# Seven products of halves in place of eight for the up projections of the second expert network

## The chip, the core and the metric

One core of a Trainium2 chip runs the whole program. The metric is device time in microseconds (us) from the first to the last instruction of one execution, with what lies around it. The engines are TensorE (PE; its weight loads are listed apart as PEld), VectorE (DVE), ScalarE (ACT), GpSimd (POOL) and SyncE (SP), which issues the DMAs.

## What is computed

Attention with a bucket mask on 2 batches of 768 tokens, then a first network, then a second one with 4 experts. Only the second network is computed in another way; `x` is the output of the first, 1536 tokens by 512.

```
h = x @ w_in ; x = (h - tanh(h)) @ w_out          # first network, d_ff = 2048
out = zeros(1536, 512)                            # second network, E = 4, F = 1024
for e in range(4):
    h = maximum(x @ w1[e], 0.0)                   # up projection, 512 -> 1024
    out += p[:, e:e+1] * (h @ w2[e])              # down projection, 1024 -> 512
```

## The kernel before

**Products in three passes.** Each 32-bit operand of the two networks is split into a high part (rounded to fp32r) and a low part (the rest), as a tile of two planes. One product of a 128x128 block with 512 columns is three matmuls: high by high, high by low, low by high. Each matmul has a weight load of its own in the PE queue.

**First network and attention: a list scheduler.** All steps up to the end of the first network are entered with `add` in a `Plan`: for each step a priority, the engines that may run it with a cost, what it reads and writes, and the buffers ("slots") that it holds. `Plan.order` then plays the steps against these costs and so fixes the order in which each engine's queue is written. At run time the engines follow these queues in order and wait on semaphores.

**Second network: written out in order.** After the planned part a plain loop follows, over experts `e`, chunks `c` of 512 tokens and blocks `fb` of 128 hidden units (4 x 3 x 8 = 96 rounds). A round has 12 matmuls for the up projection into a PSUM bank `ph` (L268 in `up_steps`: 4 blocks of the contraction by 3 passes), ACT's Relu (L959) and DVE's low part (L960) of the hidden values `hb`, and 12 matmuls for the down projection into four PSUM banks `acc` (L936). The weight blocks are split anew in every round: ACT makes the high part (L918), POOL the low part (L919). The banks `acc` sum over the 8 blocks of an expert, so DVE adds to the output only once per expert and chunk (L974, L978: 4 x 3 x 4 = 48 instructions). The output leaves by one DMA for each 128 tokens (L983). Between first and second network, ACT and DVE split the sums of the first network into high and low parts of `x` (L273, L276).

Of the kernel before, what the change touches and what calls it, by code (L numbers as in the profile page):

```python
# [16 lines left out]
P = 128  # L17
# [8 lines left out]
E = 4  # L26
# [14 lines left out]
NG = 4  # L41
NTH = 9
FILL = 8
# [169 lines left out]
def attn_moe_kernel(ctx: ExitStack, tc: tile.TileContext, qk, v, proj, ident, wa, wb, dp, out):  # L213
# [7 lines left out]
    fpa = pool("fpa", NF1)  # L221
    rwp = pool("rwp", 2)
    wps = [pool("wp0", 2)]
    hp = pool("hp", NG)
    tp2 = pool("tp2", NTH)
    apa = pool("apa", KB4)
# [15 lines left out]
    def f_tile(p):  # L242
        return p.tile([P, CH], F32, tag="f", name="f")

    def raw_tile(p):
        return p.tile([P, CH, 2], U32, tag="raw", name="raw")
# [39 lines left out]
    def banks(n, name, shape=(P, CH)):  # L286
        return tiles(n, list(shape), F32, name, pp)

    gs_ = [pair(hp, "g") for i in range(NG)]
# [19 lines left out]
        f=[f_tile(fpa) for i in range(NF1)],  # L309
        fo=[],  # L310
        raw=[raw_tile(rwp) for i in range(2)],
# [3 lines left out]
        xp=[pair(apa, "a") for kb in range(KB4)],  # L315

        g=gs_[0 : NG // 2],
        th=[tp2.tile([P, CH], F32, tag="th", name="th") for i in range(NTH)]
        + [t[:, j, :].bitcast(F32) for t in gs_[NG // 2 :] for j in range(2)],

# [4 lines left out]
        acc=[],  # L325
    )
# [400 lines left out]

    def make_xT(c, kb, p):

        pt, t = ("up", "pt", c, kb), ("xp", 1, c, kb)  # L730
# [6 lines left out]
        add(p, {TE: (0.43, turn)}, x + [("id32",)], [pt], [t])  # L737
        split(p + 0.1, lambda: pl[t], lambda: pl[pt], [pt], ("xT", c, kb), [t], psum=True)

    def network_up(c, fb, p, cut):  # L740
# [5 lines left out]
        def step(m):  # L746
            if not m:
                steps.update(enumerate(up_steps(pl[ph], pl[w], [pl["xp", 1, c, kb] for kb in range(KB4)])))
            steps[m]()

        for m in range(3 * KB4):
            add(p, {TE: (0.227, lambda m=m: step(m))},
                ks + [(("xT", c, kb), i) for kb in range(KB4) for i in ("hi", "lo")], [ph],
                [w] + [("xp", 1, c, kb) for kb in range(KB4)])
# [3 lines left out]
    def network_down(c, fb, p, cut):  # L758
# [4 lines left out]
        for db in range(4):  # L763
            add(p, {TE: (0.68, lambda db=db: down(
                pl["acc", c, db], pl[v_], pl[g], db, fb == 0, fb == NF1 - 1
            ))}, ks + gs, [("acc", c, db)], [v_, g])

# [45 lines left out]
    for i in range(SHORT):  # L813
        k = ("po", "fill", i)
        add(2e5 + i, {TE: (0.11, lambda k=k: nc.tensor.matmul(pl[k][:, 0:256], warm[:, 0:P], warm[:, 0:256], start=True, stop=True))}, (), (), [k])

# [13 lines left out]
    for c in range(NC):  # L830
# [4 lines left out]
        for db in range(4):  # L835
            split(down_at(c, NF1) - 8, lambda c=c, db=db: pl["xp", 2, c, db], lambda c=c, db=db: pl["acc", c, db],
                  [("acc", c, db)], ("x2", c, db), [("xp", 2, c, db)], psum=True)
            pl.users["xp", 2, c, db] += 1
    dps = cp.tile([P, NT // P, E], F32, name="dps")
    dsum = cp.tile([P, NT // P, 1], F32, name="dsum")  # L840
    pw = cp.tile([P, NT // P, E], F32, name="pw")
    k = [("pw",)]
    dma(330, lambda: dps, lambda: dp.rearrange("(t p) e -> p t e", p=P), w=k, lat=0.67, after=exps[-1:])
    for f in (
        lambda: nc.vector.tensor_reduce(out=dsum, in_=dps, axis=AX.X, op=ALU.add),
        lambda: nc.vector.tensor_scalar(out=dsum, in0=dsum, scalar1=1e-9, scalar2=None, op0=ALU.add),
        lambda: nc.vector.reciprocal(out=dsum, in_=dsum),
        lambda: nc.vector.tensor_tensor(out=pw, in0=dps, in1=dsum.to_broadcast([P, NT // P, E]), op=ALU.mult),
    ):
        add(331, {VE: (0.12, f)}, k, k)  # L850
    apb, fpb = [], []


# [27 lines left out]


    new = {"fo": [Slot() for i in range(NF1)], "xp": [Slot() for i in range(2 * KB4)], "raw": [Slot() for i in range(NRQ)], "wd": [Slot() for i in range(2)]}

    def switch():
        actx.close()
        wps.append(pool("wp1", 2, reuse_waits="tile"))
        rwq = pool("rwq", NRQ, reuse_waits="tile")
        apb.append(pool("apb", 2 * KB4, reuse_waits="tile"))
        fpb.append(pool("fpb", NF1, reuse_waits="tile"))  # L890
# [146 lines left out]
```

## Time and profile before

| what | value |
|---|---|
| median of 3 runs | 1003.62 us (1000.98 to 1003.82) |
| the profiled execution | 1003.25 us, of which the span of its trace is 1001.5 us |
| PE busy over the span | 986.8 us (99%), 6326 matmuls |
| PEld / DVE / ACT / POOL busy | 787.1 / 460.6 / 468.8 / 501.4 us |
| second network, 475.10 to 997.60 us of the span | 522.50 us, 2304 matmuls |

Matmuls overlap: the time of one in the table of groups is from its issue to its modelled end, so a stretch is priced by its length over the number of its matmuls and not by the mean of one. DVE and ACT rows overlap too, by some 0.08 to 0.12 us, when they stand back to back.

### The profile page before, as it was taken

To read this page: it belongs to the slowest core of one execution; us is meant where nothing else is said; L and a number is where in the kernel's file an instruction comes from. 1 tells how busy PE (TensorE), PEld (TensorE's weight loads), DVE (VectorE), ACT (ScalarE), POOL (GpSimd) and SP (SyncE) were. 2 spreads that over 40 slices of the span, in tenths; PEclk is the share of its full clock that TensorE was granted. 3 is DMA by queue.
4 is the path that set the end of the run, shared out by engine and by line. 5 is a ranking of instruction groups with operands and counts; after the bars stand their busy time and mean duration, and the time that the engine had idled before them with its cause. 6 is when DMAs were issued, how large, how long until landed. Compare 5 with 4: busy or idle time off the path is not lost.

```text
span 1001.5 us, 16255 instructions
## 1 busy us (share of the span) xinstructions
PE 986.8 (99%) x6326; PEld 787.1 (79%) x6326; DVE 460.6 (46%) x807; ACT 468.8 (47%) x941; POOL 501.4 (50%) x385
## 2 busy tenths in 40 slices
PE   8999999999999999999999999999999999999998
PEld 4766766677888888888888888888888888888886
DVE  8998998998987544444121212122121211212122
ACT  7898979887544433433333333333333333333331
POOL 3675757863654133356445444454444544444442
PEclk9999999999999999999999999999999999999999
DMA  6422243223330011123000220001300000001011
GB/s 198 128 86 81 80 145 99 78 73 114 117 116 22 22 41 44 54 84 94 1 1 1 74 85 11 1 0 53 95 21 1 1 1 1 0 1 43 1 43 42
DMA packets 32114, 53.85 MB, mean 54 GB/s; under 512 B 6150, under 2 KB 11174, under 8 KB 32038
## 3 DMA queue, kind: packets, MB, share of 16 engines
q1 hardware_dynamic: 32038, 52.83, 17.2%
q8 instruction: 49, 0.80, 0.4%
q14 instruction: 27, 0.22, 0.1%
HBM read 43.18 MB, written 3.15 MB: 46 GB/s over the span
## 4 chain that ended last, share of the span: by engine, by line
PE 89%; DVE 4%; ACT 2%; DMA 2%; issue 1%; POOL 1%; SPq 1%; POOLq 0%; DVEq 0%; ACTq 0%
PE ph L268 26%; PE acc L936 26%; PE st L255 7%; PE sf L255 7%; PE sf L268 6%; PE po L268 4%; PE st L268 2%; PE st L599 2%; PE st L604 2%; PE sf L515 2%; DVE mx L521 2%; PE po L652 1%; PE po L651 1%; PE po L653 1%; PE sf L484 1%
## 5 line engine op out<-in xcount | busy, mean ns | idle before, releaser
L919 POOL TENSOR_TENSOR w<-f,w 128x512 fp32r<-128x512 f32 x192 | 247.5, 1289 | 280.4 <-ACT w L918 280.4
L268 PE MATMUL ph<-a,w 128*128 128x512 f32 x1152 | 276.6, 389 | 0.1
L936 PE MATMUL acc<-w,hb 128*128 128x512 f32 x1152 | 276.5, 389 | 0.0
L960 DVE SCALAR_TENSOR_TENSOR hb<-ph,hb 128x512 fp32r<-128x512 f32 x96 | 66.4, 692 | 421.8 <-ACT hb L959 421.8
L268 PEld LDWEIGHTS ph<-a,w 128*128 128x128 f32 x1152 | 216.1, 188 | 45.4 <-PE st L255 0.5
L936 PEld LDWEIGHTS acc<-w,hb 128*128 128x128 f32 x1152 | 216.2, 188 | 44.9
L918 ACT ACTIVATE w<-f 128x512 fp32r<-128x512 f32 x192 | 120.5, 628 | 161.0 <-PE acc L936 108.6
L959 ACT ACTIVATE hb<-ph 128x512 fp32r<-128x512 f32 x96 | 57.4, 598 | 194.6 <-PE ph L268 194.6
L276 POOL TENSOR_TENSOR w<-f,w 128x512 fp32r<-128x512 f32 x57 | 88.4, 1551 | 114.0 <-ACT w L273 109.3
L276 POOL TENSOR_TENSOR ph<-p,ph 128x768 f16<-128x768 f32 x56 | 95.3, 1716 | 46.0 <-ACT ph L610 32.0
L521 DVE TENSOR_REDUCE mx<-sf 128x1 f32<-128x384 f32 x192 | 98.6, 549 | 9.2 <-PE sf L515 8.4
L273 ACT ACTIVATE w<-f 128x512 fp32r<-128x512 f32 x90 | 56.8, 632 | 79.7 <-PE st L255 71.4
L610 ACT ACTIVATE ph<-st 128x384 f16<-128x384 f32 x192 | 92.4, 504 | 3.1 <-PE st L604 2.8
L268 PE MATMUL sf<-a,w 128*128 128x512 f32 x288 | 77.6, 408 | 0.0
L610 ACT ACTIVATE p<-st 128x384 f32<-128x384 f32 x144 | 72.0, 500 | 5.3 <-PE st L604 4.8
L255 PE MATMUL sf<-g,w 128*128 128x512 f32 x288 | 73.8, 390 | 0.1
L255 PE MATMUL st<-g,w 128*128 128x512 f32 x288 | 73.1, 389 | 0.0
L711 POOL TENSOR_TENSOR f<-f,raw 128x512 uint32<-128x512 uint32 x32 | 48.1, 1505 | 38.0 <-DVE f L708 29.9
L599 PE MATMUL st<-qk 97*128 97x384 f16 x192 | 62.9, 327 | 2.5 <-DMA qk<-mt 1.8
L255 PEld LDWEIGHTS sf<-g,w 128*128 128x128 f32 x288 | 53.9, 188 | 11.6 <-DVE w L276 0.5
L255 PEld LDWEIGHTS st<-g,w 128*128 128x128 f32 x288 | 54.1, 188 | 11.3
L604 PE MATMUL st<-qk 128*128 128x384 f16 x192 | 62.7, 326 | 0.0
(121 smaller groups left out, 1208.0 us busy)
## 6 DMA issues: line engine op xcount, KB each, us to landing
raw<-wa SPq DMA_DIRECT2D x64, 256.0 KB
f<-wb SPq DMA_DIRECT2D x64, 256.0 KB
r<-qk SPq DMA_DIRECT2D x15, 384.0 KB
qk<-qk SPq DMA_DIRECT2D x60, 96.0 KB
vr<-v SPq DMA_DIRECT2D x8, 384.0 KB
out<-oacc SPq DMA_DIRECT2D x12, 256.0 KB
qk<-bt SPq DMA_DIRECT2D x56, 9.0 KB
r<-qk SPq DMA_DIRECT2D x2, 192.0 KB
```

Of the source, the lines that this page charges most:

```text
L255: nc.tensor.matmul(acc, a, g[:, i, :], start=(first and n == 0), stop=(last and n == 2))
L268: nc.tensor.matmul(ph, a, xt[kb][:, i, :], start=(m == 0), stop=(m == n - 1))
L276: return lambda: eng.tensor_tensor(out=dst(), in0=a(), in1=b(), op=ALU.subtract)
L521: nc.vector.tensor_reduce(out=pl["mx", h][:, qt, j : j + 1], in_=pl[ps][:, 0:384], axis=AX.X, op=ALU.max)
L599: nc.tensor.matmul(ps[j][:, 0:384], t[0:97, KB, kt * P : kt * P + P], t[0:97, QA, j * 384 : j * 384 + 384], start=True, stop=False,)
L604: nc.tensor.matmul(ps[j][:, 0:384], t[:, KC, kt * P : kt * P + P], t[:, QC, j * 384 : j * 384 + 384], start=False, stop=True,)
L610: nc.scalar.activation(o.rearrange("p (a b) -> p a b", a=2)[:, js[0]], pl[st][:, 0:384], AF.Exp, scale=1.0 / (8.0 * SC * SC),)
L918: nc.scalar.activation(w[:, 0], f, AF.Copy)
L919: nc.gpsimd.tensor_tensor(out=w[:, 1], in0=f, in1=w[:, 0].bitcast(F32), op=ALU.subtract)
L936: nc.tensor.matmul(acc[tt], a, w[:, i, :], start=(first and n == 0), stop=(last and n == 2))
L959: nc.scalar.activation(hb[:, 0, :], ph, AF.Relu)
L960: nc.vector.scalar_tensor_tensor(out=hb[:, 1, :], in0=ph, scalar=0.0, in1=hb[:, 0, :].bitcast(F32), op0=ALU.max, op1=ALU.subtract)
```

## The change

The 1024 hidden units of an expert are taken in pairs of blocks (16 pairs `u` over the experts), the contraction in two halves of 256, and the tokens of a batch `b` in two halves of `HN` = 384. The up projection of one pair and one batch is then a 2x2 by 2x2 block product. It is computed with seven block products in place of eight (the form of Strassen's algorithm with shared sums): four sums of weight halves (`stationary`), four sums of token halves (`moving`), seven products of 6 matmuls with 384 columns each (`product`), and seven additions on DVE (`plus`) that put the four hidden blocks together. These additions read a product's PSUM bank and one of three SBUF tiles `rs`. The hidden blocks are split as before (`hidden`). The down projection has the same matmuls, but its bank `dn` sums over the two blocks of a pair alone, so DVE adds to the output after every pair: 16 x 2 x 6 = 192 instructions. The steps of the second network are entered in the same `Plan` as the rest; its buffers lie where those of attention and the first network lay (`gives_later` and `hand` pass them on). The output of the first network is now copied to SBUF by ACT before it is summed and split.

```diff
+    def moving(b, p):
...
+        def cut_(o, src, i, j, r, use, p):
...
+            sums[b].append(add(p, {AC: (0.05 + n * 0.92e-3, act_copy(hi, src))}, r, [(k, "hi")], [bo[o], *use]))
+            sums[b].append(both(
+                p + 0.1, sub(nc.vector, lo, src, h32), sub(nc.gpsimd, lo, src, h32), n, [*r, (k, "hi")], [(k, "lo")], [bo[o], *use]
+            ))
...
+        for n, halves, x, y, o in ((0, (1, 0), (0, 0), (0, 1), 3), (1, (1,), (1, 0), 0, 4), (2, (0,), (1, 0), 1, 6), (3, (1, 1), (1, 0), (0, 1), 5)):
...
+    def stationary(u, p):
...
+        for n, (op, x, y, r) in enumerate((
+            (ALU.add, a21, a22, [w[1]]), (ALU.subtract, s_(0), a11, [("s", u, 0), w[0]]),
+            (ALU.subtract, a11, a21, w), (ALU.subtract, a12, s_(1), [("s", u, 1), w[0]]),
+        )):
...
+    def step2(u, b, p, q):
...
+        def product(pm, a, o):
+            def f():
+                n = 0
+                for k in range(2):
+                    hi, lo = (pl[ao][:, a, i, k * P : k * P + P] for i in range(2))
+                    for x, i in ((hi, 0), (hi, 1), (lo, 0)):
+                        nc.tensor.matmul(bank(o), x, pl["bo%d" % b, o][:, k, i, :], start=(n == 0), stop=(n == 5))
+                        n += 1
...
+        def plus(pm, o, n, to=None):
+
+            dst = (lambda: bank(o)) if to is None else (lambda: pl[rs[to]])
+            add(p + pm, {VE: (0.465, lambda: nc.vector.tensor_tensor(out=dst(), in0=bank(o), in1=pl[rs[n]], op=ALU.add))},
+                [ch[o], rs[n]], [ch[o] if to is None else rs[to]])
...
+        product(0, 0, 0)
+        add(p + 0.5, {AC: (0.37, act_copy(lambda: pl[rs[0]], lambda: bank(0)))}, [ch[0]], [rs[0]])
+        product(1, 1, 1)
+        plus(1.5, 1, 0)
+        hidden(1.6, 1, 0, 0)
+        product(2, 4, 4)
+        plus(2.5, 4, 0, 0)
+        product(4, 5, 5)
+        plus(4.5, 5, 0, 1)
+        product(6, 3, 3)
+        plus(6.5, 3, 0, 0)
+        plus(6.6, 3, 1)
+        hidden(6.7, 3, 1, 1)
+        product(8, 2, 6)
+        plus(8.5, 6, 1)
+        hidden(8.6, 6, 1, 0)
+        product(10, 6, 2)
+        plus(10.5, 2, 0)
+        hidden(10.6, 2, 0, 1)
+        for t in range(2 * HN // P):
...
+                f = lambda dn=dn, o=o, sc=sc: nc.vector.scalar_tensor_tensor(
+                    out=o(), in0=pl[dn], scalar=sc, in1=o(), op0=ALU.mult, op1=ALU.add
+                )
...
+            add(down_at(c, NF1) - 8, {AC: (0.48, lambda c=c, db=db: nc.scalar.activation(
+                xs[c][:, db, :], pl["acc", c, db], AF.Copy
+            ))}, [("acc", c, db)], [("x2", c, db)], after=turns[c] + (sums[0] if c == 2 else []))
...
+    gives_later("rs", 2, lambda: [part(hp2_t, 2 * CH + HN * i, HN) for i in range(2)], net)
...
+    for n in range(2):
+        hand("wu", n, "w2", False, ups2)
+    for n in range(4):
+        hand("up", n, "ch", False, ups2)
+        hand("acc", n, "ch" if n < 2 else "dn", False, net)
...
-    for e in range(E):
-        for c in range(NC):
-            for fb in range(NF2):
...
-                ph = up(split_w(we2[fb, 0], 0), x2[c])
```

In the rows below, line numbers of the kernel before are those of the profile; in the rows of the change L919 is a matmul of `product`, L974 a matmul of the down projection, L930 is `plus`, L940 the low part in `hidden`, L984 the addition to the output, L294 a subtraction (a low part or a sum of halves). The tiles `ab`, `xa`, `fb`, `rq`, `rw` hold the split token halves, `fa` the split weight sums, `tp` and `hp` the split hidden blocks, `hp_87` and `fb_4470` are `rs`, `xs` holds `x`, its sums and later the output. PSUM banks keep the names of attention (`sf`, `st`, `po`).

Where the last down projection of the first network (L255) ends, PE's queue had the first rounds of the second network:

```order
L255 MATMUL st_167<-g,w 128x512 x3
L255 MATMUL st_168<-g,w 128x512 x3
L268 MATMUL ph<-a,w 128x512 x24
L936 MATMUL acc_6028<-w,hb 128x512 x3
L936 MATMUL acc_6029<-w,hb 128x512 x3
```

Now seven products stand there between the last down projection of the first network (L273 in the change's numbering, same banks) and the first of the second; four products of batch 0 have moved ahead of it, in among the first network's last 11 blocks:

```order
L273 MATMUL st_145<-hp,w 128x512 x3
L273 MATMUL st_146<-hp,w 128x512 x3
L919 MATMUL sf_149<-rq,fa 128x384 x6
L919 MATMUL sf_148<-ab,fa 128x384 x6
L919 MATMUL po_151<-rw,fa 128x384 x6
L919 MATMUL po_150<-xa,fa 128x384 x6
L919 MATMUL st_144<-xa,fa 128x384 x6
L919 MATMUL po_150<-fb,fa 128x384 x6
L919 MATMUL sf_147<-fb,fa 128x384 x6
L974 MATMUL st_145<-w,tp 128x512 x6
```

The rounds with their up projection first are gone from here; the first down projection of the second network comes after seven products in place of 24 matmuls.

At the same place DVE's queue had the four low parts of the last chunk of `x` and went on with one instruction a round:

```order
L276 TENSOR_TENSOR a<-sf_171,a 128x512
L276 TENSOR_TENSOR a<-sf_170,a 128x512
L276 TENSOR_TENSOR a<-st_167,a 128x512
L276 TENSOR_TENSOR a<-st_168,a 128x512
L960 SCALAR_TENSOR_TENSOR hb<-ph,hb 128x512 x9
```

Now 22 instructions stand between the first sum of token halves and the last low part of batch 0's hidden blocks. The first nine are two sums of 512 and 256 elements, a sum of 768, three low parts of 768 (all for batch 1), a `plus` of batch 0, the low part of a weight block (512) and another sum of 768; these are the next twelve:

```order
L940 SCALAR_TENSOR_TENSOR tp<-po_150,tp 128x384
L294 TENSOR_TENSOR fb<-xs_99,fb 128x2x384
L930 TENSOR_TENSOR hp_87<-st_144,hp_87 128x384
L294 TENSOR_TENSOR w<-hp_87,w 128x512
L930 TENSOR_TENSOR fb_4470<-sf_147,hp_87 128x384
L294 TENSOR_TENSOR fb<-xs_99,fb 128x2x384
L930 TENSOR_TENSOR hp_87<-sf_149,hp_87 128x384
L930 TENSOR_TENSOR sf_148<-sf_148,fb_4470 128x384
L930 TENSOR_TENSOR sf_149<-sf_149,fb_4470 128x384
L930 TENSOR_TENSOR po_151<-po_151,hp_87 128x384
L940 SCALAR_TENSOR_TENSOR tp<-sf_148,tp 128x384
L940 SCALAR_TENSOR_TENSOR tp<-sf_149,tp 128x384
```

The additions of batch 0 have come in among the splits for batch 1; the low part in the last of these rows is one that the first down projection of the second network reads.

In the middle of the second network, where PE's queue repeated 12 matmuls L268 and 12 matmuls L936, one step (one pair, one batch) begins so; the down projections are those of the step before:

```order
L919 MATMUL sf_149<-ab,fa 128x384 x6
L919 MATMUL st_144<-ab,fa 128x384 x6
L919 MATMUL po_151<-ab,fa 128x384 x6
L974 MATMUL st_145<-w,tp 128x512 x3
L974 MATMUL st_145<-w,hp 128x512 x3
L919 MATMUL po_150<-ab,fa 128x384 x6
L974 MATMUL st_146<-w,tp 128x512 x3
L974 MATMUL st_146<-w,hp 128x512 x3
L919 MATMUL sf_147<-rq,fa 128x384 x6
```

It goes on in turn with down projections three and four and the last two products, and ends with down projections five and six side by side. The two banks of the down projection, `st_145` and `st_146`, alternate; products use the other six banks.

## Rows read from the trace of the kernel before

**Rows 1.** The page: span, busy time of PE, and the span in 40 slices.

```profile
span 1001.5 us, 16255 instructions
...
PE   8999999999999999999999999999999999999998
...
PEclk9999999999999999999999999999999999999999
```

**Rows 2.** Busy time by stretch: us, then each engine's busy us, PE clock, DMA.

```profile
475.10:997.60 522.50, 522.48 (x2304) 432.34 (x2304) 98.61 (x145) 166.66 (x286) 243.59 (x189) 1.00 0.07 21
```

**Rows 3.** Groups by line and shape: count | busy us, mean ns | idle before.

```profile
L268 PE MATMUL ph<-a,w 128*128 128x512 f32 x1152 | 276.6, 389 | 0.1
L936 PE MATMUL acc<-w,hb 128*128 128x512 f32 x1152 | 276.5, 389 | 0.0
L268 PEld LDWEIGHTS ph<-a,w 128*128 128x128 f32 x1152 | 216.1, 188 | 45.4 <-PE st L255 0.5
```

**Rows 4.** Timeline of PE, f16 matmuls alone: start us, us from first start to last end.

```profile
182.24 0.33 PE L599 MATMUL st<-qk 97*128 97x384 f16 x1
182.41 0.33 PE L604 MATMUL st<-qk 128*128 128x384 f16 x1
```

**Rows 5.** Timeline of PE, a 384-column matmul followed by 32-bit weights (two places).

```profile
182.57 0.33 PE L515 MATMUL sf<-qk 96*128 96x384 f16 x1
182.60 0.76 PE L268 MATMUL sf<-a,w 128*128 128x512 f32 x2
183.19 0.34 PE L515 MATMUL sf<-qk 96*128 96x384 f16 x1
...
156.09 0.34 PE L515 MATMUL sf<-qk 96*128 96x384 f16 x1
156.13 1.00 PE L268 MATMUL sf<-a,w 128*128 128x512 f32 x3
156.97 0.34 PE L599 MATMUL st<-qk 97*128 97x384 f16 x1
```

**Rows 6.** Timeline of the weight loads: 32-bit ones that follow each other closely.

```profile
182.57 0.36 PEld L268 LDWEIGHTS sf<-a,w 128*128 128x128 f32 x2
...
250.04 0.47 PEld L734 LDWEIGHTS st<-id,xs 128*128 128x128 f32 x4
```

**Rows 7.** Timeline of DVE: back-to-back rows of 384 and of 512 elements.

```profile
101.54 1.94 DVE L521 TENSOR_REDUCE mx<-sf 128x1 f32<-128x384 f32 x4
...
995.60 2.79 DVE L978 SCALAR_TENSOR_TENSOR oacc<-acc,pw,oacc 128x512 f32<-128x512 f32 x4 [2.08 <-PE acc L936]
```

**Rows 8.** Groups of DVE, ACT and POOL whose shapes are near those of the change.

```profile
L626 DVE TENSOR_TENSOR ph<-st,ph 128x384 f16<-128x384 f32 x48 | 24.5, 548 | 0.6 <-ACT st L623 0.4
L276 DVE TENSOR_TENSOR ph<-p,ph 128x768 f16<-128x768 f32 x16 | 16.5, 1035 | 2.3 <-ACT ph L610 2.3
L276 DVE TENSOR_TENSOR g<-th,g 128x512 fp32r<-128x512 f32 x36 | 26.2, 727 | 1.3 <-ACT g L273 0.5
L276 DVE TENSOR_TENSOR w<-f,w 128x512 fp32r<-128x512 f32 x39 | 31.9, 819 | 4.2 <-ACT w L273 2.2 <-POOL f L711 1.2 <-DVE w L719 0.5
L623 ACT ACTIVATE st<-st 128x384 f32<-128x384 f32 x48 | 21.9, 499 | 0.0
L919 POOL TENSOR_TENSOR w<-f,w 128x512 fp32r<-128x512 f32 x192 | 247.5, 1289 | 280.4 <-ACT w L918 280.4
L276 POOL TENSOR_TENSOR w<-f,w 128x512 fp32r<-128x512 f32 x57 | 88.4, 1551 | 114.0 <-ACT w L273 109.3 <-issue 1.6 <-DVE w L719 1.3
```

**Rows 9.** Timeline from the first network to the second, and the last evacuations there.

```profile
473.45 1.52 PE L255 MATMUL st<-g,w 128*128 128x512 f32 x6
...
474.33 1.28 ACT L273 ACTIVATE a<-st 128x512 fp32r<-128x512 f32 x2
474.96 1.37 DVE L276 TENSOR_TENSOR a<-st,a 128x512 fp32r<-128x512 f32 x2
475.12 5.69 PE L268 MATMUL ph<-a,w 128*128 128x512 f32 x24
```

**Rows 10.** Timeline of the end.

```profile
992.00 5.60 PE L936 MATMUL acc<-w,hb 128*128 128x512 f32 x24
...
996.38 2.37 SPq L983 DMA_DIRECT2D out<-oacc  x4
```

More of the change, by code (lines that the diff above doesn't have):

```diff
@@ L40 @@
 N32 = 3
-NG = 4
 NTH = 9
+HN = S // 2
+MV = 2 * 2 * HN
+NU = E * NF2 // 2
 FILL = 8
@@ L238, in attn_moe_kernel, with part, pairs, singles @@
     xs = [xo.tile([P, 4, DM], F32, tag="xo", name=f"xs{c}") for c in range(NC)]
[L242 to L246, printed above, removed]
+    def part(t, at, n):
+        return t[:, at : at + n]
+    def pairs(t, at, n):
+        return [part(t, at + 2 * CH * i, 2 * CH).rearrange("p (a b) -> p a b", a=2) for i in range(n)]
+    def singles(t, at, n):
+        return [part(t, at + CH * i, CH) for i in range(n)]
+    def raws(t):
+        return [part(t, 2 * CH * i, 2 * CH).rearrange("p (c w) -> p c w", w=2) for i in range(2)]
     def pair(p, tag):
@@ L726, in split, with xp_of @@
         return [(w, "hi"), (w, "lo")]
+    turns = [[] for c in range(NC)]
+    def xp_of(c):
+        return "xp1" if c == 1 else "xp"
     def make_xT(c, kb, p):
-        pt, t = ("up", "pt", c, kb), ("xp", 1, c, kb)
+        pt, t = ("up", "pt", c, kb), (xp_of(c), c, kb)
         def turn():
@@ L747, in step @@
             if not m:
-                steps.update(enumerate(up_steps(pl[ph], pl[w], [pl["xp", 1, c, kb] for kb in range(KB4)])))
+                steps.update(enumerate(up_steps(pl[ph], pl[w], [pl[xp_of(c), c, kb] for kb in range(KB4)])))
             steps[m]()
@@ L766, in network_down, with movers, pieces @@
             ))}, ks + gs, [("acc", c, db)], [v_, g])
+    HN2 = 2 * HN
+    def movers(t, at, n):
+        return [part(t, at + MV * i, MV).rearrange("p (k i n) -> p k i n", k=2, i=2) for i in range(n)]
+    def pieces(b, *halves):
+        cuts_, at = {0, HN}, [HN2 * b + HN * s for s in halves]
+        for t in at:
+            cuts_ |= {c * CH - t for c in range(NC) if 0 < c * CH - t < HN}
+        cuts_ = sorted(cuts_)
+        return [(i, j, [divmod(t + i, CH) for t in at]) for i, j in zip(cuts_, cuts_[1:])]
@@ L769, in attn_moe_kernel, with second @@
+    def second():
+        p0 = 780
+        for u in range(NU):
+            stationary(u, p0 + 40 * u - (30 if u else 60))
+            for b in range(B):
+                step2(u, b, p0 + 40 * u + 20 * b, p0 + 40 * u + 20 * b + 20)
     nc.vector.memset(warm, 0.0)
@@ L835, in attn_moe_kernel @@
         for db in range(4):
[L836 to L851, printed above, removed]
+            add(down_at(c, NF1) - 8, {AC: (0.48, lambda c=c, db=db: nc.scalar.activation(
+                xs[c][:, db, :], pl["acc", c, db], AF.Copy
+            ))}, [("acc", c, db)], [("x2", c, db)], after=turns[c] + (sums[0] if c == 2 else []))
+        if c == 1:
+            moving(0, down_at(c, NF1))
+    moving(1, down_at(2, NF1) - 6)
+    second()
     def give(cls, *made):
@@ L931, in down2 @@
-    def down2(acc, w, g, first, last):
-        for tt in range(4):
-            hi = g[:, 0, tt * P : tt * P + P]
-            lo = g[:, 1, tt * P : tt * P + P]
-            for n, (a, i) in enumerate(((hi, 0), (hi, 1), (lo, 0))):
-                nc.tensor.matmul(acc[tt], a, w[:, i, :], start=(first and n == 0), stop=(last and n == 2))
-    def accs():
-        return [acp.tile([P, CH], F32, tag="acc", name=f"acc{i}") for i in range(4)]
-    def flush(keep=0):
-        while len(pend) > keep:
-            pend.pop(0)()
@@ L986, in attn_moe_kernel @@
-    flush()
 def kernel(**inputs):
```

255 lines of the change are left out of this document (183 added, 72 removed).

## The prediction

> **What bounds the kernel now.** I read the page first: PE is busy in nearly every one of the 40 slices, and the granted clock stands at its upper level, 2.4 GHz, in all of them [rows 1]. Then the busy times by stretch: the second network takes 522.50 us, PE is busy for 522.48 of these, and it runs 2304 matmuls in them [rows 2]. No other engine is busy for half of that time (POOL 243.59 us). So PE's queue sets the end, each of its matmuls of 512 columns takes 522.50 / 2304 = 0.2268 us of it, and only fewer or shorter matmuls can give time back. Last, the groups by line: the up projection (L268) and the down projection (L936) have 1152 matmuls each [rows 3], so each is 1152 x 0.2268 = 261.3 us. Nothing idles in front of them. The question is thus what a matmul of 384 columns costs with 32-bit operands, and whether the work that the seven products bring to DVE and ACT leaves PE waiting.
>
> **The matmuls.** The down projection keeps its 1152 matmuls: 0 us. The up projection becomes 16 pairs x 2 batches x 7 products x 6 = 1344 matmuls of 384 columns. No row shows one with 32-bit operands; the trace has 384 columns in f16 alone, and those follow each other every 0.165 us [rows 4], which is one column per clock at 2.4 GHz (0.160 us) and 5 ns more. At the same rate 512 columns are 0.2133 us, so the 32-bit matmul has 0.0135 us beside its columns. I take that rest as fixed: 0.160 + 0.0135 = 0.1735 us, in all 1344 x 0.1735 = 233.2 us, 28.1 us less than 261.3. If the rest grew with the columns it would be 0.170 us and 4.6 us less again.
>
> Bounds from the nearest rows. Where an f16 matmul of 384 columns stands ahead of 32-bit ones, the weights of these are loaded behind it. From 182.57 to 183.19 us, 0.62 us, there are one of 384 columns and two of 512: 0.62 - 2 x 0.2268 = 0.166 us for the short one. From 156.09 to 156.97, 0.88 us, with three of 512: 0.88 - 0.680 = 0.20 us [rows 5]. So a product's matmul costs 0.166 to 0.20 us, the up projection 223.1 to 268.8. I stay at 0.1735, near the lower end: both places also pay for changing between f16 and 32 bit, which the products don't. The weight loads allow it: the second of two 32-bit loads that last 0.19 us each ended 0.36 us after the first began, so it began 0.17 us after the first, and four loads fit in 0.47 us [rows 6].
>
> **The start of the second network.** Before, PE goes from one network to the other with a gap of 0.3 us: its last six matmuls start at 473.45 and take 6 x 0.2268, the next starts at 475.12 [rows 9]. The up projection of chunk 0 needs nothing from the last chunk. In the change the queue has seven products between the last down projection of the first network and the first of the second: 42 x 0.1735 = 7.3 us. The first down projection needs hidden blocks of batch 0, whose low parts stand at the end of 22 DVE instructions; the four products that were pulled ahead cost nothing but wait in their banks. DVE's third instruction needs the last evacuation by ACT, which in the trace ends 0.8 us after PE's last matmul (474.33 + 1.28 against 474.81) [rows 9]. From there to the low part that is needed there are 19 instructions. Seven are of 768 elements: 1.035 us alone [rows 8], 0.95 back to back (rows of 384 elements last 0.548 but follow each other every 0.465, since four take 1.94 [rows 7, 8]). Ten are of 384 with an operand in PSUM: 0.465. Two are of 512 in SBUF: 0.727 less the same overlap, 0.64. Together 6.65 + 4.65 + 1.28 = 12.6 us, so PE gets its block at 0.9 + 12.6 + 0.1 = 13.6 us and has work for 7.3: it stands for 6.3 us. ACT has to make the high halves in between, some of which DVE will meet not ready; I take **6.5 us**. Bounds: 5 us if the splits run like the f16 ones without any wait, 10 if DVE is slowed by POOL throughout (0.819 in place of 0.727 [rows 8]) and `plus`, whose results the next one reads, keeps its full 0.548. The old gap of 0.3 us falls away.
>
> **The end of the first network.** POOL makes the low parts of the last weight blocks, 1.29 to 1.55 us each [rows 8], and now some sums of token and weight halves between them. A block lasts 12 x 0.2268 = 2.7 us on PE, and its weight buffer is renewed within that. One sum of 256 elements in the way is half of 1.29, 0.65 us. The four products that stand between the last 11 blocks cover part of that; I take 0.5 us, from 0 to 2.
>
> **A step in the middle.** One pair and one batch are 42 products' matmuls and 36 of the down projection, 42 x 0.1735 + 36 x 0.2268 = 15.45 us, a pair 30.9. DVE has for a pair 14 `plus` and 8 low parts of 384 (22 x 0.465 = 10.2 us), 12 additions to the output (0.68 each at most, from four in 2.79 us [rows 7]: 8.2) and 3.2 us of weight sums and splits: 21.6 us, 70% of PE's time. Before, these additions were 48 in all and are now 192; the 144 more cost nothing while DVE has this spare. `plus` writes PSUM, which no DVE row shows; ACT in PSUM and out of it took 0.499 us [rows 8], no more than elsewhere. I walked a step through PE's and DVE's queues with these durations. Products come back to a bank that was freed more than 5 us earlier. The tightest place is the pair of banks of the down projection: the sixth one follows the fourth in its bank with one product (1.04 us) and one down projection (1.36) between, 2.4 us, and the addition that frees it ends 1.2 us before it is needed. So 0 us, with a cover of 1.2. POOL goes from 192 low parts of weight blocks to four short instructions a pair, and SP's queue moves the same blocks of weights, 64 in all, a pair ahead of their use: 0 us for both.
>
> **The end.** Last matmul to the end of the span is 3.9 us now (992.00 + 5.60 [rows 10]). The last addition and its DMA stay. The last six down projections stand alone and the first of them follows a DVE queue that waits once for ACT: 0.2 us.
>
> **Sum.** Against the profiled execution's own 1003.25 us (the median is 1003.62): -28.1 + 6.5 - 0.3 + 0.5 + 0.2 = -21.2, so **982 us**.
>
> **Rivals.** *The weight loads set the pace (slower).* A load lasts 188 ns [rows 3], longer than the 173.5 ns of the matmul meant to hide it. If a product's matmul could only start when its load has wholly ended, it would cost 0.19 to 0.20 us: at 0.20 the up projection is 268.8 us, +7.5 in place of -28.1, and with the same +6.9 for start and end the time is 1018. It turns at 0.189 us a matmul, where the 6.9 are just paid. Against it: the loads that began 0.17 us apart and the 0.166 us of rows 5 and 6. The Trainium skill (Perfetto Trace Analysis, Identifying the Most-Contended Engine) says to judge TensorE's headroom by the share of time in weight loads and not by matmul busy time; by that rule the products, with 188 ns of load in each 173.5, would be over full and this rival would come true. 7 in 100.
>
> *The product's matmul is cheaper.* At the lower bound of 0.166 us the up projection is 223.1 us and the time 1003.25 - 38.2 + 6.9 = 972. For it: the first place of rows 5; against it: 0.0135 us beside the columns in every row of 512. The Trainium skill (TensorE: Matmul & The Clock Gate, Back-to-back issue gap) gives N / 2.4 + 2.5 ns for a lone matmul, an estimate of 162.5 ns for 384 and 215.8 for 512; this trace has 226.8 for 512, so it doesn't bear the rule out, and by it the time would be 967. 12 in 100.
>
> *DVE comes late in every step.* Each `plus` and Relu crosses between engines, and a pair has 14 and 8 of these in one queue. If the addition that frees a down bank comes 1.2 us later than my walk has it, each further 0.5 us costs 32 x 0.5 = 16 us: 998. For it: 70% load and POOL's sums beside it; against: the cover. 8 in 100.
>
> **How the numbers follow.** The forecast holds 73 in 100, with its own range 976 to 988 (PE standing for 5 to 10 us, 0.170 to 0.1755 us a matmul). The range takes in the cheaper matmul and most of late DVE: 970 to 994. A measurement here tells 0.3% from no change, some 3 us. Faster by more: forecast, cheaper matmul and most of late DVE, 0.91. Within: weight loads near 0.19 and the rest of late DVE, 0.04. Slower: weight loads above it, 0.05.
>
> **What would show it.** The products' matmuls start 0.173 us apart in the timeline (0.19 or more: weight loads; 0.166: cheaper). PE idles 5 to 10 us in the 14 us after the last matmul of the first network, behind DVE's L294, L930 and L940, and then not until the end; repeated gaps ahead of L974 with DVE as their releaser would be the late DVE. Up to some 290 us nothing differs. It would be wrong if a product costs more than 0.18 us, or if the queue's order, laid out with costs of its own, leaves gaps in the last blocks of the first network.

## The result, and the profile after

The changed kernel takes 988.27 us (median of 4 runs, 987.91 to 989.68) where the kernel before took 1003.11 beside it (4 runs): a ratio of 0.9858, 95% interval 0.984 to 0.9877. It is faster, by 15 us where 21 were forecast; 982 was too low. 988.27 lies inside the range of 970 to 994, and just above the narrower 976 to 988 that the forecast had given itself. The profiled execution of the changed kernel took 987.91 us, its span is 986.1.

The page of the changed kernel, the lines that answer to [rows 1]:

```profile
span 986.1 us, 17092 instructions
...
PE 967.8 (98%) x6518; PEld 806.8 (82%) x6518; DVE 765.7 (78%) x1293; ACT 438.4 (44%) x909; POOL 325.9 (33%) x270
...
PE   8999999999999999999899999999999999999998
...
DVE  7999998998988664488787777777777777777665
...
PEclk9999999999999999999899999999999999999999
```

PE still fills the span. There is one blemish, and it is the same in both PE rows: the slice from 468 to 493 us, in which the second network starts. The stretches, with the columns of [rows 2] (from:to, us, then busy us and instructions of PE, PEld, DVE, ACT and POOL, PE clock, DMA share, GB/s):

```profile
478.54:492.93 14.39, 9.88 (x43) 8.84 (x42) 13.38 (x19) 9.36 (x17) 7.74 (x6) 0.76 0.18 55
483.92:490.75 6.83, 4.09 (x12) 3.70 (x13) 6.07 (x9) 3.71 (x6) 3.48 (x3) 0.50 0.28 84
500.00:950.00 450.00, 450.00 (x2247) 405.02 (x2246) 336.12 (x557) 113.44 (x214) 47.74 (x54) 1.00 0.10 31
```

The first is from the end of the first network's last matmul to the start of the first down projection: 14.39 us for 42 products that need 42 x 0.1735 = 7.29, so 7.1 us are lost: PE stands for 4.51 us (14.39 less 9.88 busy), and most of the rest is two groups of products at a slower clock. In the second row, a part of the first, the clock is at its lower level, 1.2 GHz (0.50). The third is the steady state: PE never idle, 2247 matmuls in 450 us, of which two reach in from before. A step of 42 products and 36 down matmuls is 78 x 450 / 2245 = 15.63 us, and I had worked out 15.45. Over 32 steps the difference is 5.8 us. VectorE is busy for 336.12 of 450 us, 75%; I had said 70.

Where the 0.18 us of a step are, the timeline of PE shows (start us, us from first start to last end, line, operation, tiles, shape, count):

```profile
717.11 1.21 PE L919 MATMUL sf<-fb,fa 128*128 128x384 f32 x6
718.15 1.55 PE L974 MATMUL st<-w,tp 128*128 128x512 f32 x6
719.54 1.21 PE L919 MATMUL sf<-fb,fa 128*128 128x384 f32 x6
720.58 2.92 PE L974 MATMUL st<-w,tp 128*128 128x512 f32 x12
```

From start to start, six products (L919) take 718.15 - 717.11 = 1.04 us, 0.1733 each. The six down matmuls (L974) take 719.54 - 718.15 = 1.39 us, 0.2317 each, where before each took 0.2268 [rows 2]. From 500 to 960 us the down matmul's mean from start to start is 0.2310 us, the product's 0.1744. And it isn't noise: a group of six down matmuls that stands between two products takes 229, 233, 236, 224, 231 and 236 ns from matmul to matmul, to a nanosecond or so, in all 116 such groups from 500 to 960 us.

The sum by its own steps, measured in the two profiled executions:

| step | forecast us | measured us | from |
|---|---|---|---|
| products in place of the up projection | -28.1 | -26.9 | 1344 x 0.1744 = 234.4 against 261.3 |
| down projection | 0 | +4.7 | 1152 x 0.2309 = 266.0 against 261.3 |
| start of the second network | +6.5 | +7.1 | 14.39 - 7.29 |
| the old gap | -0.3 | -0.3 | [rows 9] |
| end of the first network | +0.5 | +0.4 | one place at 441 us, PE behind a low part on DVE |
| end | +0.2 | +0.3 | 0.33 at 973 us; from the last matmul's end 3.84 us, before 3.87 |
| sum | -21.2 | -14.7 | the times: 987.91 - 1003.25 = -15.3 |

The remaining 0.6 us lie ahead of the second network, in work that the change doesn't touch. There the executions of these kernels differ by up to 4.9 us: the 2501st matmul starts at 209.43 us here, at 210.56 in the trace of before, and at 209.37 to 214.23 in the runs below, in two of which the clock was at 1.2 GHz for a few microseconds between 134 and 169 us. So small differences are also read from the end of the first network to the last matmul: 503.6 us here.

Two questions are left: why a down matmul takes longer although nothing in it changed, and whether the start of the second network costs what it does for the reason that I gave.

### The profile page after: what moved, and what is told of

It reads as the page before. It is cut to its first block, busy times and chain, and to the rows that moved or that the text cites. A ratio compares the mean times of both kernels' runs of the same rounds, so it can differ in the third digit from the quotient of the medians.

```text
span 986.1 us, 17092 instructions
## 1 busy us (share of the span) xinstructions
PE 967.8 (98%) x6518; PEld 806.8 (82%) x6518; DVE 765.7 (78%) x1293; ACT 438.4 (44%) x909; POOL 325.9 (33%) x270
## 4 chain that ended last, share of the span: by engine, by line
PE 89%; DVE 5%; DMA 2%; ACT 2%; issue 1%; POOL 1%; SPq 0%; POOLq 0%; ACTq 0%; DVEq 0%
PE st L974 27%; PE sf L919 12%; PE po L919 8%; PE sf L273 6%; PE st L273 6%; PE sf L286 5%; PE po L286 4%; PE st L919 3%; PE st L619 3%; PE st L286 2%; PE sf L535 2%; PE st L624 2%; DVE mx L541 2%; PE po L672 1%; PE po L671 1%; PE po L673 1%
## 5 line engine op out<-in xcount | busy, mean ns | idle before, releaser
L974 PE MATMUL st<-w,tp 128*128 128x512 f32 x864 | 228.3, 393 | 0.1
L974 PEld LDWEIGHTS st<-w,tp 128*128 128x128 f32 x864 | 159.8, 188 | 24.3 <-issue 0.5
L984 DVE SCALAR_TENSOR_TENSOR xs<-st,pw,xs 128x512 f32<-128x512 f32 x180 | 134.5, 747 | 50.9 <-PE st L974 50.8
L294 POOL TENSOR_TENSOR ph<-p,ph 128x768 f16<-128x768 f32 x56 | 95.2, 1714 | 46.3 <-ACT ph L630 34.8
L974 PE MATMUL st<-w,hp 128*128 128x512 f32 x288 | 81.6, 392 | 0.0
L294 POOL TENSOR_TENSOR w<-hp,w 128x512 fp32r<-128x512 f32 x16 | 21.4, 1337 | 180.0 <-ACT w L291 180.0
L273 PE MATMUL sf<-hp,w 128*128 128x512 f32 x288 | 73.9, 391 | 0.2
L273 PE MATMUL st<-hp,w 128*128 128x512 f32 x288 | 73.3, 389 | 0.0
L294 POOL TENSOR_TENSOR w<-fb,w 128x512 fp32r<-128x512 f32 x28 | 44.9, 1603 | 62.0 <-ACT w L291 59.7
L974 PEld LDWEIGHTS st<-w,hp 128*128 128x128 f32 x288 | 54.0, 188 | 12.6
L273 PEld LDWEIGHTS sf<-hp,w 128*128 128x128 f32 x288 | 53.8, 188 | 11.8 <-DVE hp L294 0.6
L273 PEld LDWEIGHTS st<-hp,w 128*128 128x128 f32 x288 | 54.1, 188 | 11.4
L294 POOL TENSOR_TENSOR fa<-ab,fa 128x256 fp32r<-128x256 f32 x15 | 11.5, 768 | 155.7 <-ACT fa L291 146.2
L286 PE MATMUL sf<-xa,w 128*128 128x512 f32 x228 | 62.7, 414 | 0.0
L671 PE MATMUL po<-v,ph 128*128 128x65 f16 x576 | 61.7, 192 | 0.0
L672 PE MATMUL po<-v,ph 128*128 128x64 f16 x576 | 61.6, 195 | 0.0
L673 PE MATMUL po<-v,ph 128*128 128x65 f16 x576 | 61.4, 191 | 0.0
```

The lines of the kernel that those rows point to most:

```text
L273: nc.tensor.matmul(acc, a, g[:, i, :], start=(first and n == 0), stop=(last and n == 2))
L286: nc.tensor.matmul(ph, a, xt[kb][:, i, :], start=(m == 0), stop=(m == n - 1))
L294: return lambda: eng.tensor_tensor(out=dst(), in0=a(), in1=b(), op=ALU.subtract)
L671: nc.tensor.matmul(o[:, c : c + D + 1], hi, vt[:, kt, 0 : D + 1], start=(kt == 0 and qt == 0), stop=False)
L672: nc.tensor.matmul(o[:, c : c + D], hi, vt[:, kt, D + 1 : 2 * D + 1], start=False, stop=False)
L974: nc.tensor.matmul(pl[dn], x, w[:, y, :], start=(n == 0), stop=(n == 5))
```

## Experiment 1: the two kinds of groups with nothing else running

**Theories.** A: the down matmul is slower because the matmuls ahead of it are shorter, a matter of TensorE alone. B: VectorE, now at 75%, gets in the way in the banks or in memory. C: the new places of the operands. The bench issues the same two groups from fixed tiles, in stretches of 72 to 156 matmuls:

```
+        for n, kind in enumerate('dpdpdpdpdpdpdp'):
+            if kind == 'p':
+                fs, o, w = prod(gp_), pb[gp_ % 6], HN; gp_ += 1
+            else:
+                w = HN if kind == 'n' else CH; fs, o = down(gd, w), pd[gd % 2]; gd += 1
+            for f in fs:
+                d = f()
+                nc.tensor.matmul(*mm(d), start=d['start'], stop=d['stop'])
```

(`down` and `prod` yield the six matmuls of a group as the changed kernel writes them; the other stretches have other strings, and some a copy on DVE behind each group.)

> A kernel that computes nothing of the reference: it only runs stretches of six-matmul groups of the second network's two forms (down: 512 columns; product: 384 columns) with no other engine at work unless the stretch says so, and writes a constant as output. In the trace of the changed kernel a down matmul takes 0.2310 us from start to start where one took 0.2268 before, always the same at the same place of a group. Theory A, the change of length: 512 alone 0.2268, 384 alone 0.1735, down groups between product groups 0.231 with nothing else running, and the same or less in longer blocks (two and two, six and seven); down matmuls cut to 384 columns between products 0.1735. Theory B, VectorE reading the banks or the memory beside it: alternating groups alone 0.2268, 0.231 only in the stretches where VectorE reads each group's bank or copies in the memory beside. Theory C, the operands of the down groups themselves: 0.231 for 512 alone too.

Three stretches (512 alone, 384 alone, six and six in turns; the columns as above, and a count can hold a neighbour or two of the stretch):

```profile
19.27:35.59 16.32, 16.32 (x74) 13.51 (x73) 0.00 (x0) 15.91 (x15) 0.00 (x0) 1.00 0.00 1
35.59:48.09 12.50, 12.50 (x73) 12.50 (x72) 0.00 (x0) 0.13 (x1) 0.00 (x0) 1.00 0.00 0
48.09:65.13 17.04, 17.04 (x86) 15.19 (x86) 0.00 (x0) 0.00 (x0) 0.00 (x0) 1.00 0.00 1
```

Alone, 72 matmuls of 512 take 16.32 us, 0.2267 each, and 72 of 384 take 12.50, 0.1737. (The 15.91 us of ScalarE in the first row are copies that were meant to run in the last stretch and ran ahead. They cost the matmuls nothing: in experiment 2, 512 alone takes 16.32 us with ScalarE idle.) In turns, 42 of each should take 9.52 + 7.30 = 16.82 us and take 17.04, while no other engine does anything:

```profile
50.52 1.55 PE L291 MATMUL pd<-w,h 128*128 128x512 f32 x6
51.91 1.21 PE L291 MATMUL pb<-bo,ao 128*128 128x384 f32 x6
52.96 1.55 PE L291 MATMUL pd<-w,h 128*128 128x512 f32 x6
```

The six of 512 take 51.91 - 50.52 = 1.39 us, as in the changed kernel, and from matmul to matmul 229, 233, 236, 224, 231 and 236 ns, the kernel's very row, mean 0.2315. With VectorE reading the bank of every group: 0.2315. With VectorE copying in memory beside: 0.2308. With 512 alone and VectorE reading: 0.2267. With the same down groups cut to 384 columns between products: 0.1736. With the groups in the order of the changed kernel's steps: 0.2310 for 512 and 0.1740 for 384, where the kernel has 0.2310 and 0.1744. So A holds and B falls. C has nothing left to explain: the bench's tiles lie in other places than the kernel's and show the same row.

## Experiment 2: which lengths, and how long the effect lasts

All lengths here come from the same tiles, so that only the length changes:

```
+        for n, w in enumerate(([384] * 6 + [512] * 6) * 7):
+            d = [f for f in down(n // 6 % 6)][n % 6]()
+            nc.tensor.matmul(pd[n // 6 % 2][:, 0:w], d["lhsT"], w2[n % 2][:, n % 3 % 2, 0:w], start=True, stop=True)
```

and so for one length alone, and for blocks of 1, 3, 12, 24 and 48.

> Like the first bench, computes nothing of the reference: stretches of matmuls on 32-bit operands alone, first of one length each (512 to 128 columns), then blocks of 384 and 512 columns in turns, the blocks 1, 3, 6, 12, 24 and 48 matmuls long, then blocks of 6 of 448 or 256 against 512. From 0.2267 at 512 and 0.1737 at 384 a straight line gives 0.200 at 448, 0.147 at 320, 0.120 at 256 and 0.068 at 128; the recorded weight load of 0.188 would be a floor under all but 448 and 512 if it set the pace (already not so at 384), a shorter floor would show as a flat end below some length. Blocks: the first bench lost 32 ns for each pair of blocks of 6 and 65 ns for each pair of 12. Theory 1, a fixed cost for a change of length: the same loss for each pair at any block length. Theory 2, the loss sits in the matmuls behind a change and dies out: it grows with the block length and stands still from about 12 to 18 matmuls. Theory 3, every matmul in a mixed stretch is slow: it grows with the length without end.

Stretches of 256, 192 and 128 columns alone, then of blocks of 12, 24 and 48 in turns:

```profile
74.48:83.11 8.63, 8.63 (x74) 8.63 (x73) 0.00 (x0) 0.00 (x0) 0.00 (x0) 1.00 0.00 0
83.11:91.13 8.02, 8.02 (x74) 8.02 (x73) 0.00 (x0) 0.00 (x0) 0.00 (x0) 1.00 0.01 2
91.13:99.14 8.01, 8.01 (x74) 8.01 (x73) 0.00 (x0) 0.00 (x0) 0.00 (x0) 1.00 0.00 0
...
145.79:165.23 19.44, 19.44 (x97) 17.40 (x96) 0.00 (x0) 0.00 (x0) 0.00 (x0) 1.00 0.00 1
165.23:194.23 29.00, 29.00 (x145) 26.07 (x144) 0.00 (x0) 0.00 (x0) 0.00 (x0) 1.00 0.00 1
194.23:232.77 38.54, 38.54 (x194) 34.71 (x193) 0.00 (x0) 0.00 (x0) 0.00 (x0) 1.00 0.00 0
```

The loss is what a stretch takes beyond its matmuls at the spacing that they have well behind a change, 226.7 ns at 512 and 173.3 at 384. For one pair of blocks it is 15 ns with blocks of 1, 24 with 3, 33 with 6, 61 with 12, 67 with 24 and 67 with 48. Theory 2 holds: the loss sits behind a change of length, in the first nine matmuls of 512 and the first seven of 384, and is used up after about 12. Neither a fixed price for each change nor a price for each matmul fits. 448 against 512 loses 17 ns a pair of blocks of 6, 256 against 512 20 ns, so each of the three changes of length that I tried does it. What in TensorE makes it stays open.

The lengths alone, from 512 down to 128 in steps of 64, in ns: 226.7, 202.7, 173.7, 146.6, 119.9, 111.4 and 111.3. The forecast's line (one column per clock and 13.5 ns) holds at 384, 320 and 256, and is 2.5 ns low at 448. Below 256 there is a floor of 0.111 us, 72 matmuls in 8.02 and in 8.01 us. The recorded weight load of 0.188 us is no floor. The Trainium skill (TensorE: Matmul & The Clock Gate, LDWEIGHTS (loading the stationary operand)) gives a load P / 1.2 ns for P columns, an estimate of 107 ns here, and the bench's floor is near it.

## Experiment 3: fewer changes of length in the kernel itself

```
-            add(q + (2, 5, 7, 8, 11, 12)[t], {TE: (1.362, down3)},
+            add(q + (12.1, 12.2, 12.3, 12.4, 12.5, 12.6)[t], {TE: (1.362, down3)},
```

(and the same due times, half a unit on, for the additions to the output).

> The changed kernel with the due times of the six down groups of a step set together, so that the plan places six down groups and then about seven products in place of one and one in turns. Theory A (a change of length slows the down matmuls): their mean falls from 0.2310 to 0.2275 to 0.229 us, which is 1152 x 0.002 to 0.0035 = 2.3 to 4 us: 984.3 to 986. Theory B (VectorE beside it): 0.231 stays and the time too, 987.5 to 989. Theory C (the operands): the same as B. Against all: six down groups in a row make VectorE write six outputs in a row with two banks, so TensorE may wait for a bank: 990 or more.

The plan now mostly places six or seven products and then four to six down groups. The steady state:

```profile
500.00:950.00 450.00, 450.00 (x2260) 406.52 (x2259) 335.74 (x546) 111.15 (x214) 90.33 (x68) 1.00 0.10 31
```

2260 matmuls in place of 2247 in the same 450 us, with VectorE as busy as before (335.74). The down matmul's mean is 0.2287 us in place of 0.2310, or 0.2281 without one short pause in nearly every pair, 0.05 us each; the product's is 0.1742 in place of 0.1744. From the end of the first network to the last matmul it takes 501.4 us in place of 503.6: 2.2 us, at the lower end of what theory A gave. The median is 987.26 us (ratio 0.9843, 0.983 to 0.9857), outside the 984.3 to 986 that I expected under A, and only 1 us better than the change, which the medians alone could not tell. In the profiled execution the missing part lies ahead of the second network: the 2501st matmul starts 1.7 us later than in the change. So the evidence is the spacing of the matmuls: the order of groups moves the down matmul's time with VectorE's load as it was. A again.

## Experiment 4: the start of the second network, by the due time of the second batch's operands alone

In the change the second batch's moving operands have an earlier due time than the first step, so VectorE makes them first (ScalarE and GpSimd, which have a share in them, too). One number puts them behind it:

```
-    moving(1, down_at(2, NF1) - 6)
+    moving(1, down_at(2, NF1) + 55)
```

> The changed kernel with one number changed: the due time of the second batch's moving operands is put 61 later, behind the first batch's first step, so that VectorE's queue has the first step's additions and low parts ahead of them. Theory: the 7 us that TensorE lost at the start of the second network came of VectorE's queue order (and the clock's fall of what TensorE waited there): 988.3 becomes 982 to 983, no wait over 1 us of a product on L930/L940 in the 15 us after the first network, granted clock 1.0 there. Rival 1: the same VectorE work only waits elsewhere (the first output additions may not write before the second batch's sums are made, so the down groups stall): 986 to 988. Rival 2: the clock falls anyway there, and the gain is the waits alone: 984.5 to 985.5.

PE of the changed kernel first, then of this one (columns of the timeline, and in brackets the idle time before and who ended it):

```profile
478.54 1.23 PE L919 MATMUL sf<-rq,fa 128*128 128x384 f32 x6
479.60 1.20 PE L919 MATMUL sf<-ab,fa 128*128 128x384 f32 x6
482.48 1.34 PE L919 MATMUL po<-rw,fa 128*128 128x384 f32 x6 [1.67 <-ACT hp L291]
486.66 2.29 PE L919 MATMUL po<-xa,fa 128*128 128x384 f32 x6 [2.84 <-DVE tp L940]
488.83 2.18 PE L919 MATMUL st<-xa,fa 128*128 128x384 f32 x6
490.85 1.20 PE L919 MATMUL po<-fb,fa 128*128 128x384 f32 x6
491.89 1.20 PE L919 MATMUL sf<-fb,fa 128*128 128x384 f32 x6
492.93 2.92 PE L974 MATMUL st<-w,tp 128*128 128x512 f32 x12
```

```profile
480.56 1.21 PE L919 MATMUL po<-rw,fa 128*128 128x384 f32 x6
481.61 1.20 PE L919 MATMUL st<-xa,fa 128*128 128x384 f32 x6
...
486.17 1.55 PE L974 MATMUL st<-w,tp 128*128 128x512 f32 x6
487.56 0.33 PE L919 MATMUL sf<-fb,fa 128*128 128x384 f32 x1
488.18 1.14 PE L919 MATMUL sf<-fb,fa 128*128 128x384 f32 x5 [0.29 <-POOL fb L294]
```

In the change, PE waits twice. The first wait ends with ScalarE, which had made high parts for the second batch before it emptied a bank. The second ends with a low part at 486.61 us, and up to there VectorE had gone through its queue from 478.01 without a pause of 0.3 us. Two groups of products run mostly at 1.2 GHz (2.29 and 2.18 us, where others take 1.20). Here the products follow each other and the first down group starts 6.8 us sooner. The clock stays at 2.4 GHz. The same stretch of 14.54 us of the one and the other:

```profile
478.54:493.08 14.54, 10.03 (x44) 8.99 (x43) 13.53 (x20) 9.51 (x17) 7.74 (x6) 0.77 0.18 55
```

```profile
478.46:493.00 14.54, 14.15 (x76) 12.93 (x75) 14.01 (x20) 10.06 (x19) 13.65 (x9) 1.00 0.20 57
```

VectorE works as much in both (13.53 and 14.01 us); PE runs 76 matmuls in place of 44. The time is 982.28 us (ratio 0.9804, 0.979 to 0.9817), 6 us below the change, and 498.0 in place of 503.6 us from the end of the first network. So it was the order of this work, in VectorE's queue above all, and what was put off found room later: rival 1 falls, and rival 2 with it. Gaps of some 1.7 us in all are left from 484 to 497 us. Whether the clock had a part in the 7.1 us this can't tell, since waits and clock went together.

## Experiment 5: the clock held, the waits left

```
+    for i in range(30):
+        k = ("dn", "fill", i)
+        add(3e5 + i, {TE: (0.22, lambda k=k: nc.tensor.matmul(pl[k], warm[:, 0:P], warm, start=True, stop=True))}, (), (), [k])
```

> The changed kernel with 30 extra matmuls of 16-bit zeros (0.216 us each, 6.5 us in all, into the two free output banks, results unused) where the plan leaves TensorE idle at the start of the second network. The granted clock should stay 1.0 there. Theory: of the 7 us lost, 2.2 us are the two product groups that ran at 1.2 GHz; VectorE stood idle behind them, so with the clock held the first down group starts 1 to 2.2 us earlier: 986 to 987.3. Rival: VectorE's queue sets the end of the stretch alone (13.6 us by its own work), the slow products fell into waits: 987.5 to 988.5. Rival 2: the extra matmuls themselves get in the way: 989 or more.

The stretch from the end of the first network to the first down group, to be set against the 14.39 us at clock 0.76 above:

```profile
480.24:495.00 14.76, 13.96 (x73) 9.84 (x72) 14.07 (x21) 10.16 (x18) 7.76 (x6) 1.00 0.18 57
```

The clock is held, and the first down group starts no sooner: after 14.76 us. But the fillers themselves end this stretch. PE, then VectorE, of this run, and VectorE of the change:

```profile
492.84 1.21 PE L919 MATMUL sf<-fb,fa 128*128 128x384 f32 x6
493.88 1.47 PE L1089 MATMUL st<-warm 128*128 128x512 f16 x6
495.00 3.12 PE L974 MATMUL st<-w,tp 128*128 128x512 f32 x12
```

```profile
494.28 1.00 DVE L940 SCALAR_TENSOR_TENSOR tp<-sf,tp 128x384 fp32r<-128x384 f32 x2
```

```profile
492.98 1.01 DVE L940 SCALAR_TENSOR_TENSOR tp<-sf,tp 128x384 fp32r<-128x384 f32 x2
```

The last product ends 493.88 - 480.24 = 13.64 us into the stretch, and then six fillers stand ahead of the down group. What VectorE has to give for this group is the second of the two low parts; the group's sixth matmul reads it. It is ready 15.04 us into the stretch here (494.28 + 1.00 - 480.24), and 15.45 in the change (492.98 + 1.01 - 478.54). So the fall of the clock cost VectorE's queue some 0.4 us, and no more than about that could be won by holding it: the slow products had mostly filled waits. My theory of 1 to 2.2 us for the clock falls. The rival holds but for these 0.4 us, which were not won here: PE ran the sixth matmul 1.07 us after its operand was ready, and 0.1 us in the change. So rival 2 has a part too.

The time is 990.15 us (ratio 0.9869, 0.9856 to 0.9883), 2 us above the change where I expected none, though the two intervals overlap. 0.5 us of that lie behind the first network (504.1 us in place of 503.6), and that is the fillers. In the profiled execution the rest lies ahead of it, where both kernels issue the same instructions, so I don't put it down to them.

## Experiment 6: the new order of work without the seven products

```
-        for n, (o, kh, s) in enumerate(((0, 0, 0), (1, 1, 0))):
+        for n, (o, kh, s) in enumerate(((0, 0, 0), (1, 1, 0), (3, 0, 1), (2, 1, 1))):
...
-        tt = [("tt%d" % b, n) for n in range(4)]
...
-        product(1, 1, 1)
-        plus(1.5, 1, 0)
-        hidden(1.6, 1, 0, 0)
...
+        for o, (i, s) in enumerate(((0, 0), (1, 0), (0, 1), (1, 1))):
+            product(3 * o, i, s, o)
+            hidden(3 * o + 2.5, o, i, s)
```

(The sums of token halves and of weight halves go, and every `plus`; each of the four `product` calls now issues two plain products, 12 matmuls, into one bank.)

> One part of the change alone: the second network in the list scheduler with halves of 384 columns, but with the eight plain products of halves (two accumulate in one bank) in place of seven with sums. 1536 product matmuls in place of 1344: at 0.1744 that is 267.9 in place of 234.4 us, +33.5. VectorE loses the additions, so the start of the second network should cost about 1 us in place of 7: 988.3 + 33.5 - 6 = 1016 if the down matmuls stay at 0.231 (theories A and C), 1011 if they fall to 0.2268 since VectorE has less to do (theory B). Rival: most of the gain came of the scheduler, not of the seven products; then this is at 1003 or below.

1014.3 us (ratio 1.0116, 1.0097 to 1.0134): slower than before, and 26 us slower than the change. The steady state:

```profile
500.00:950.00 450.00, 450.00 (x2268) 407.82 (x2267) 213.36 (x298) 83.06 (x160) 33.99 (x27) 1.00 0.09 31
```

VectorE is down to 213.36 us, and PE doesn't wait at the start of the second network. The time lies between the 1016 of theories A and C and the 1011 of B; what decides is that the down matmul still takes 0.2310 us, with VectorE at less than half load. The product takes 0.1742. Eight products are 1536 x 0.1742 = 267.6 us, 6.3 more than the 261.3 of before, and the down matmuls 4.7: 11.0, against the 11.4 measured. So scheduler and halves alone cost time, and the rival (1003 or below) falls. All the gain is the eighth product left out: 192 x 0.1744 = 33.5 us, less the 7 of the start that come with the sums.

## Experiments 7 and 8: a better version

Experiment 7 joins the edits of experiments 3 and 4. Experiment 8 adds a new order of the first steps, so that the first batch's second step stands ahead of the second batch's first:

```
-                step2(u, b, p0 + 40 * u + 20 * b, p0 + 40 * u + 20 * b + 20)
+                at = p0 + 20 * {(0, 1): 2, (1, 0): 1}.get((u, b), 2 * u + b)
+                step2(u, b, at, at + 20)
```

It also has the second pair's weight sums due 15 earlier.

> Both single changes so far in one kernel: the second batch's operands due later (982.28 alone) and the six down groups due together (down matmul 0.2281 in place of 0.2310, 3.3 us by that, 1.0 us in the medians). If the two are independent: 979 to 981. Rival: the later operands leave VectorE with a backlog that the grouped downs, with two banks, wait for: 982 or more.

> As the kernel with both, and also the order of the first four steps changed, so that the first batch's second step stands ahead of the second batch's first (7 us more of TensorE work ahead of the second batch's operands). What was left of waits at the start of the second network with the later operands was 1.5 us (gaps of a product at 484.6, 487.6, 494.5 and 496.0): 0.5 to 1.2 us less than the kernel with both, 978 to 980. Rival: the first two steps' output additions wait for the second batch's sums either way, no difference.

981.06 us (ratio 0.9784, 0.9767 to 0.9802) and 981.34 us (0.9785, 0.9772 to 0.9798). From the end of the first network to the last matmul they take 495.7 and 494.8 us, after 498.0 with experiment 4's edit alone: the two edits add up, 5.6 and 2.3 us in place of 5.6 and 2.2, and the third gives 0.9, each read from one profiled execution. I had expected medians of 979 to 981 and of 978 to 980: the first is missed by less than 0.1 us, the second by 1.3. In the medians the three can't be told apart, since the work ahead of the second network varies by more. All three are faster than the change: their intervals end at 0.9817, 0.9802 and 0.9798, and that of the change begins at 0.984.

## Why the prediction was right, and where not

**What bounds the kernel** was read rightly. PE's queue set the end before and sets it after, and outside the start of the second network only matmul time counted.

**The product's matmul** was the step with the most at stake and the most exact: 0.1735 us forecast from the f16 rows, 0.1737 alone on the bench (0.1733 well behind its start), 0.1744 in the kernel. The 0.9 ns between forecast and kernel are the change of length. Staying near the lower end of 0.166 to 0.20 [rows 4, 5] was right, but the reason given, that both places also paid for a change of the operands' type, is not shown: 0.166 is no more than the 0.165 of f16 alone, and no run tests a change of type by itself.

**"The down projection keeps its 1152 matmuls: 0 us"** is the step that failed. It cost 4.7 us, with the 1.2 of the products nearly the whole of the gap to the forecast. I took a duration from rows in which every matmul has 512 columns [rows 2, 3] and used it for a queue in which lengths alternate. The bounds of that step were one number, so it was luck that the range held the time, by the room that I had left for other things. Rows 5 may have held a hint: the same short matmul came out at 0.166 and at 0.20 us by what stood beside it, and I put that on the short matmul alone.

**The start of the second network**: forecast 6.5, measured 7.1, and the count of VectorE's queue, 13.6 us to the first down group, came within 0.8 of the 14.39. Its reason is shown by experiment 4: the second batch's operands stood ahead of the first step's, in VectorE's queue above all. That the numbers are so near is partly luck. I had counted 13.5 us to the end of the low part, and it came after 15.45 (15.04 with the clock held): VectorE also paused for ScalarE's high parts (0.44 and 0.32 us), and some of its rows took longer than I had priced them. But the down group began 1.06 us ahead of it, since only its sixth matmul reads it, and I had PE wait for it with the whole group. I did not foresee the fall of the clock; by experiment 5 it cost some 0.4 us.

**The middle**: no stall there, as walked. The cover of the down banks held at 75% load, and even with six down groups in a row the banks cost no more than a few hundredths of a microsecond a step.

**Ends**: 0.5 and 0.2 forecast, 0.4 and 0.3 measured. The releaser at 441 us is not POOL, which I named, but a low part on DVE.

**The rivals.** *Weight loads set the pace* is refuted: products start 0.1744 us apart with loads that record 0.188. The recorded loads fill 82% of the span, and on the bench 100% (12.50 of 12.50 us) with the matmuls 0.1737 us apart. The Trainium skill (Perfetto Trace Analysis, Identifying the Most-Contended Engine) would judge TensorE's headroom by the share of weight loads, beside the share of peak FLOPs. By that share the bench had none left, and yet the columns set its pace. *Cheaper products* came to 0.1737 even alone, not 0.166. *DVE late in every step* didn't come: PE's 450.00 busy of 450.00 us.

## What to carry to other kernels

A matmul's duration taken from a uniform stretch holds only there: where lengths alternate in TensorE's queue, price the neighbours too, and place groups of one length together. When an algebraic trick moves work to VectorE, a full pipeline hides it and the start doesn't, so look at which of its pieces the first consumer needs and put the others behind them. A slow clock inside a wait can cost little (some 0.4 us of the 7.1 here): find what ends the stretch before paying to keep the clock up, and count that the matmuls which hold it stand in the queue too.

## What the runs showed of the hardware that I had not expected

- A change between matmul lengths slows the matmuls behind it, in the same pattern each time, with no other engine at work: 512 columns between blocks of six of 384 take 229, 233, 236, 224, 231 and 236 ns in place of 226.7. The loss dies out within some 12 matmuls, at 67 ns for a pair of blocks.
- 32-bit matmuls with a fresh 128-column weight load each follow each other every 119.9 ns at 256 columns and every 111.4 and 111.3 at 192 and 128, while each load is recorded with 188 ns.
- The granted clock went to 1.2 GHz for 6.83 us from 483.92 us, after TensorE had stood for 1.67 us, run six products and stood for the first 0.1 us of a second wait of 2.84 us, and it stayed there over the 12 matmuls that ran in that stretch.
